# Second-layer weights of a two-layer block: converted inside the first layer's passes, in half chunks, instead of beside attention

## The chip, the cores and the metric

The kernel runs on one core of a Trainium2 chip. A core has a matrix engine (PE, with its weight loads listed apart as PEld), a vector engine (DVE), an activation engine (ACT), a general engine (POOL) and a queue engine (SP) that issues the DMAs. Each engine runs its own instructions in order; between engines only semaphores order the work. Matrix products land in PSUM, everything else lies in SBUF or, in DRAM, in tensors of the kernel.

The metric is the device time of one execution in microseconds (us). The kernel before takes 1280.64 us, the median of three runs (1280.03 to 1281.29).

## The reference

Two blocks follow each other. Attention over 64 pairs of batch and head (576 queries and keys of width 64), where only scores within `tau` of the row's maximum are kept; then a feed-forward layer over the 4608 tokens, 512 to 2048 to 512, with a squared ReLU between.

```python
scores = 0.125 * q @ k.T                      # per batch and head
scores = where(scores >= max(scores) - tau, scores, -1e9)
attn   = softmax(scores) @ v                  # float32
x      = attn as (4608, 512)                  # heads side by side
h      = maximum(x @ w_in, 0)                 # w_in (512, 2048), float64 in DRAM
out    = (h * h) @ w_out                      # w_out (2048, 512), float64 in DRAM
```

The two weight matrices arrive as float64. The core computes in float32, so each weight is turned from the two 32-bit words of a float64 into a float32 by integer arithmetic on the engines.

## The kernel before, in words

The program has three stages, one after the other: attention, the first layer, the second layer.

**Attention** is a software pipeline of periods: `period(p)` works on two units of 128 queries, and the order of its steps is written out by hand as a list of names. There are two lists that matter here. `PLAIN` has the attention steps, and one step `s1` that adds or subtracts two weight tiles on POOL. `CONVERTING` has the attention steps and `c1` to `c6`, which convert one chunk of weights; a period takes this list when a chunk is under way in it (`converts(p)`). `starts` gives chunk m the periods m+2 and m+3. Each period has one reciprocal (L488), so their starts mark the periods in the trace.

A chunk is 128 rows of 512 float64 values, 512 KB. Its six steps are: the high words' absolute value on ACT (L208), a conversion of the low words on ACT (L214), a clamp on POOL (L221), a shift and mask on DVE (L229), a merge of sign and exponent bits on DVE (L237), and the sum of the two parts on POOL (L248). Before, 32 chunks are converted so: 16 of the first layer's matrix, which stay in SBUF (`wall`), and 16 of the second layer's, which are stored to a DRAM tensor `w` (L250), since SBUF has no room for them yet.

**Both layers** use a scheme with fewer products than the plain block product: a 4 x 4 split of the matrices is multiplied with 7 x 7 = 49 products of blocks in place of 64, and pays with sums and differences of blocks. `OUTER` is the order of the seven outer kinds. So each weight matrix is needed in 49 blocks: 16 raw ones and 33 made by subtracting. For the first layer they are made during attention by `sums` (44 sums, step `s1`; what is left at its end goes to DVE and into the first pass). For the second layer they are made in DRAM during the first layer by `chain_out`: a chain loads four blocks of a quarter's width from `w` (L1192), makes four new ones from them with four subtractions of 128 x 128 on POOL (L125) and stores these (L1197). There are 44 chains, 16 along one side (raw blocks only) and 28 along the other. In the last pass of the first layer, `reload` fetches the 49 finished blocks from `w` into `wall`.

**The first layer** runs nine passes (`PASSES`) of 49 products each. Three passes work on 512 tokens and six are halves of a 1024-token set. After each product comes a tick: `also` runs what is planned for that tick of the pass (weight chains, loads of later tokens, sums of later tokens), all in the program's order. One outer kind is seven products (`inner`): PE writes a product into one of six PSUM banks, and DVE adds it to what is there from before (L128, PSUM plus SBUF to SBUF, 128 x 512); the first of each seven is copied by ACT (L769). Some of the results go on to POOL, which adds them to the running sums (L128, SBUF plus SBUF, 128 x 512). PE writes the bank of the third product of the seven again at the sixth, and that of the fourth again at the seventh, so DVE has to have read them by then. Finished results are squared by ACT (L916, L917) and stored to DRAM by SP.

The sums of later tokens (`sum_v`) run on DVE too (L125), after ACT has copied one of the two operands into PSUM (L879, tile `c`). DVE thus reads one operand from PSUM and one from SBUF in all its work of this stage. POOL reads both operands from SBUF.

**The second layer** runs nine blocks of 49 products (L1085) with the weights in `wall`.

## Time and profile before

| what | value |
|---|---|
| time, median of three runs | 1280.64 us (1280.03 to 1281.29) |
| profiled execution, span of its instructions | 1278.6 us |
| attention, up to the first product of the first layer | 492.6 us |
| first layer, first to last product | 387.9 us |
| PE, share of the span | 98% |
| DVE, ACT, POOL, share of the span | 78%, 67%, 70% |
| granted PE clock | 1.00 |

The profile gives the profiled execution its span, 1278.6 us from its first instruction to its last; the 2.0 us between this and the median of the runs lie around it. Busy times of an engine are the time in which at least one of its instructions ran. In rows of groups the columns are line, engine, operation, output and inputs, shapes and count, then busy time in us and mean length of one in ns, then the engine's idle time just before and what ended it. Rows of windows give a stretch, its length, and for each engine the busy time in it with the count of its instructions.

### The profile page before, as it was taken

The numbers are of one execution on the slowest core, as the hardware profiler recorded it, in microseconds if no ns is written. First come the engines' busy times: TensorE is split into PE (matmuls) and PEld (weight loads), VectorE is DVE, ScalarE is ACT, GpSimd is POOL, SyncE is SP. The second block draws the span as 40 slices with busy tenths as digits, with TensorE's granted clock in tenths as the row PEclk, the third lists the DMA queues.
The fourth block names the chain that finished last, engine by engine and source line by source line (L and its number), as shares of the span: only waits on it lengthen the run. The fifth ranks groups of instructions, "written<-read, shape, count | busy, mean of one in ns | idle before, by whom it ended". The sixth has DMA issues, their size and how long they took to land.

```text
span 1278.6 us, 44201 instructions
## 1 busy us (share of the span) xinstructions
PE 1255.2 (98%) x17459; PEld 1087.0 (85%) x17459; DVE 1000.2 (78%) x2449; ACT 855.6 (67%) x1552; POOL 897.4 (70%) x1094
## 2 busy tenths in 40 slices
PE   8999999999999999999999999999999999999998
PEld 6666666677777768988888888999999999999998
DVE  6999999999999997787878877877645664565463
ACT  6999999999999995666765767667422441343240
POOL 2565665655555557888798889858877777786775
PEclk9999999999999999999999999999999999999999
DMA  6566666544333413457666666589635414522511
GB/s 155 152 158 160 165 193 182 151 94 112 89 83 84 97 34 98 156 164 219 198 190 204 192 198 187 177 324 394 208 122 166 133 50 149 166 95 76 161 35 34
DMA packets 256591, 191.89 MB, mean 150 GB/s; under 512 B 96000, under 2 KB 217344, under 8 KB 256384
## 3 DMA queue, kind: packets, MB, share of 16 engines
q1 hardware_dynamic: 254928, 188.63, 49.8%
q8 instruction: 137, 2.24, 0.7%
q14 instruction: 70, 0.57, 0.1%
q10 hardware_dynamic: 1456, 0.44, 0.1%
HBM read 116.65 MB, written 72.35 MB: 148 GB/s over the span
## 4 chain that ended last, share of the span: by engine, by line
PE 70%; DMA 1%; ACT 1%; DVE 1%; issue 1%; ACTq 0%; DVEq 0%; SPq 0%
PE po L1085 30%; PE ph L946 27%; PE sc L544 5%; PE sc L445 4%; PE pt L388 2%; DMA wall<-w 1%; PE sc L406 1%; PE sc L388 1%; DVE arena L128 1%; DVE arena L463 0%; DMA g<-arena 0%; ACT arena L916 0%; ACT c L879 0%; DMA arena<-xT 0%; ACT arena L917 0%
## 5 line engine op out<-in xcount | busy, mean ns | idle before, releaser
L128 POOL TENSOR_TENSOR arena<-arena 128x512 f32<-128x512 f32 (+1 forms) x314 | 377.7, 1222 | 126.3 <-DVE arena L128 89.4
L1085 PE MATMUL po<-wall,arena 128*128 128x128 f32 x3528 | 394.4, 275 | 0.2 <-DVE arena L125 0.2
L1085 PEld LDWEIGHTS po<-wall,arena 128*128 128x128 f32 x3528 | 394.1, 192 | 0.4 <-DVE arena L125 0.4
L946 PE MATMUL ph<-arena,wall 128*128 128x128 f32 (+1 forms) x2352 | 387.4, 327 | 1.1 <-DVE arena L665 0.5
L946 PEld LDWEIGHTS ph<-arena,wall 128*128 128x128 f32 x2352 | 354.2, 191 | 34.2 <-DVE arena L128 2.2
L128 DVE TENSOR_TENSOR arena<-ph,arena 128x512 f32<-128x512 f32 x378 | 255.6, 688 | 75.8 <-PE ph L946 50.0
L125 POOL TENSOR_TENSOR arena<-arena 128x128 f32<-128x128 f32 (+2 forms) x314 | 255.2, 814 | 29.1 <-DMA arena<-w 10.7
L879 ACT COPY c<-arena 128x512 f32<-128x512 f32 (+2 forms) x319 | 176.1, 558 | 104.2 <-DVE arena L125 85.7
L473 ACT ACTIVATE arena<-arena 128x576 f32<-128x576 f32 x288 | 232.1, 918 | 16.7 <-DVE arena L463 16.7
L128 DVE TENSOR_TENSOR arena<-po,arena 128x128 f32<-128x128 f32 x378 | 108.3, 290 | 168.0 <-PE po L1085 167.4
L478 DVE SCALAR_TENSOR_TENSOR arena<-arena 128x576 f32<-128x576 f32 x288 | 225.5, 811 | 0.4 <-POOL arena L470 0.4
L463 DVE TENSOR_SCALAR_CACHE_REDUCE arena<-sc 128x576 f32<-128x576 f32 x288 | 204.5, 751 | 14.3 <-ACT arena L535 6.4
L125 DVE TENSOR_TENSOR arena<-arena,c 128x512 f32<-128x512 f32 (+2 forms) x283 | 176.8, 633 | 7.9 <-ACT c L879 6.1
L544 PEld LDWEIGHTS sc<-arena 64*64 64x64 f32 x5760 | 144.4, 133 | 43.1 <-DVE arena L463 39.1
L445 PE MATMUL sc<-arena 64*64 64x64 f32 (+1 forms) x2304 | 170.0, 415 | 0.3 <-DVE arena L665 0.3
L544 PE MATMUL sc<-arena 64*64 64x128 f32 (+1 forms) x5760 | 160.8, 262 | 8.5 <-DVE arena L463 5.8
L535 ACT COPY arena<-pt 128x1024 f32<-128x1024 f32 x144 | 166.0, 1153 | 1.6 <-PE pt L388 1.5
L769 ACT COPY arena<-po 128x128 f32<-128x128 f32 x63 | 16.6, 264 | 185.4 <-PE po L1085 185.4
L388 PEld LDWEIGHTS pt<-ident,arena 64*128 64x128 f32 x2304 | 83.0, 138 | 41.7 <-ACT arena L535 33.8
L388 PE MATMUL pt<-ident,arena 64*128 64x64 f32 x2304 | 100.8, 227 | 2.4 <-ACT arena L535 2.1
L445 PEld LDWEIGHTS sc<-arena 64*64 64x64 f32 x2304 | 62.5, 132 | 47.5 <-issue 22.7
L470 POOL TENSOR_SCALAR arena<-arena,tau_p 128x2 f32<-128x2 f32 x144 | 65.5, 455 | 41.8 <-DVE arena L463 35.2
(51 smaller groups left out, 936.6 us busy)
## 6 DMA issues: line engine op xcount, KB each, us to landing
g<-arena SPq DMA_DIRECT2D x144, 256.0 KB, 2.6
arena<-g SPq DMA_DIRECT2D x144, 256.0 KB, 4.5
w<-arena SPq DMA_DIRECT2D x60, 256.0 KB, 2.8
wall<-w SPq DMA_DIRECT2D x49, 256.0 KB, 5.3
arena<-w SPq DMA_DIRECT2D x44, 256.0 KB, 3.1
arena<-in_v_dram SPq DMA_DIRECT2D x32, 288.0 KB, 4.6
out_dram<-arena SPq DMA_DIRECT2D x70, 128.0 KB, 2.4
arena<-in_q_dram SPq DMA_DIRECT2D x64, 128.0 KB, 4.1
```

Source lines behind the costliest of these rows:

```text
L125: e.tensor_tensor(out=out, in0=x, in1=y, op=ALU.subtract)
L128: e.tensor_tensor(out=out, in0=x, in1=y, op=ALU.add)
L388: made = nc.tensor.transpose(pt[:, r, ts(slot, HALF)], of[rows, :], ident[rows, rows])
L445: made = nc.tensor.matmul(sc[at, ds(to, count)], lhs, kT[rows, ds(at_k, count)], start=True, stop=True)
L463: made = nc.vector.tensor_scalar(out=s[:, j, :], in0=sc[:, ds(at, S)], scalar1=1.0, scalar2=None, op0=ALU.mult, op1=ALU.min, accum_out=nmx ...
L473: nc.scalar.activation(out=w[:, :, j, :], in_=of(j), func=AF.Exp, bias=nmx[:, j : j + 1], scale=-1.0)
L478: nc.vector.scalar_tensor_tensor(out=w[:, :, j, :], in0=of(j), scalar=thr[:, j : j + 1], in1=w[:, :, j, :], op0=ALU.is_le, op1=ALU.mult, a ...
L535: touch("weights", nc.scalar.copy(joined(to), whole(pt, 0, count)), at, 2 * BANK, m)
L544: made = nc.tensor.matmul(sc[ds(u * D, D), ds(5 * j * BANK + row, count)], loaded_v[i][rows, (c - (u != j)) % CH, :], wT[m][rows, ds(weigh ...
L879: nc.scalar.copy(c, y)
L946: nc.tensor.matmul(to[:, j, :], W_IN[m, k][:, ts(h * parts_ + j, P)], x_of(m, k), start=(not more and j == 0), stop=True, skip_group_check ...
L1085: nc.tensor.matmul(to, g[:, j, :], w[:, j, :], start=(not more and j == 0), stop=(j == 3), skip_group_check=True)
```

## The change

All conversion of the second layer's matrix leaves attention: only the 16 chunks of the first layer are left there, so the last `CONVERTING` period is the 17th of these and not the 33rd, and `PLAIN` periods follow 16 periods sooner.

In the first layer's passes a new function `half_step` converts the matrix in 32 half chunks, one each ten ticks from tick 8 on (`EVERY`). A half chunk is four raw blocks at one place along the other side, 64 columns wide, 128 x 256 values in all. In order of ticks: 0, absolute value and low words on ACT; 1, clamp, shift and mask, and merge, all three on DVE, from SBUF to SBUF; 2, the sum on POOL; 3, the load of the next half by SP; 4, the store of the four raw blocks and a copy of three of them into PSUM (`c`) by ACT; 5, three differences or sums on DVE that make the four new blocks; 6, their store. The loads have one buffer (`raw_w`), the results one each (`new_w`, `made_w`).

The 16 chains along the first side go, since the half steps make these blocks. The 28 others stay, at new ticks (92 to 368 and not 153 to 367), and their four subtractions are arranged another way. `RAW` and `MADE`, the places of the blocks in `w`, are reordered to suit.

```diff
-    RAW, MADE = (7, 1, 3, 2), (7, 5, 6, 4)
+    RAW, MADE = (1, 7, 2, 3), (5, 7, 4, 6)
...
-    blocks_out = [(m, k) for k in RAW for m in RAW]
-    chunks += [(W_OUT, m, k, out_blocks[m, k]) for m, k in blocks_out[:EARLY]]
...
-    starts = {m + 2: m for m in range(16 + EARLY)}
+    starts = {m + 2: m for m in range(len(chunks))}
...
+        def half_step(j, s_):
+            lo, hi = (raw_w.rearrange("p m (c two) -> p m c two", two=2)[:, :, :, z] for z in range(2))
+            bits = new_w.bitcast(I32)
+            if s_ == 0 and is_wide:
+                nc.scalar.activation(out=new_w, in_=hi.bitcast(FP32), func=AF.Abs)
+                nc.scalar.activation(out=lo, in_=lo.bitcast(U32), func=AF.Copy, bias=0.0, scale=2.0**-29)
+            if s_ == 1 and is_wide:
+                low, high = (0x38000000, 0x47EFFFFF)
+                nc.vector.tensor_scalar(
+                    out=new_w, in0=new_w, scalar1=as_float(high), scalar2=as_float(low), op0=ALU.min, op1=ALU.max
+                )
+                nc.vector.tensor_scalar(
+                    out=bits, in0=bits, scalar1=3, scalar2=0x3FFFFFFF, op0=ALU.logical_shift_left, op1=ALU.bitwise_and
+                )
+                nc.vector.scalar_tensor_tensor(
+                    out=hi, in0=hi, scalar=-(1 << 30), in1=bits, op0=ALU.bitwise_and, op1=ALU.bitwise_or
+                )
+            if s_ == 2 and is_wide:
+                nc.gpsimd.tensor_tensor(out=bits, in0=hi, in1=lo, op=ALU.add)
+            if s_ == 3 and j + 1 < len(halves_w):
+                load_half(j + 1)
+            if s_ == 4:
+                nc.sync.dma_start(out=to_w(0, j), in_=new_w)
+                c = b_pool.tile([P, BANK], FP32, tag="b", name="c")[:, 0 : 3 * HALF_C].rearrange("p (m c) -> p m c", m=3)
+                nc.scalar.copy(c, new_w[:, 0:3, :])
+                where_w[j] = c
+            if s_ == 5:
+                c = where_w.pop(j)
+                minus(nc.vector, made_w[:, 0:2, :], new_w[:, 1:4:2, :], c[:, 0:2, :])
+                plus(nc.vector, made_w[:, 3, :], made_w[:, 1, :], c[:, 0, :])
+                minus(nc.vector, made_w[:, 2, :], c[:, 2, :], made_w[:, 3, :])
+            if s_ == 6:
+                nc.sync.dma_start(out=to_w(4, j), in_=made_w)
...
-        chains = [((0, RAW.index(k)), c) for k in RAW for c in range(4)]
-        chains += [((1, made_at(m)), c) for c in range(4) for m in OUTER]
-        BEGINS = (0, 6, 12, 18, 24, 43)
-        CHAINS = [49 * n + BEGINS[c] for n in range(NSTEP - 1) for c in range(3 if n == 0 else 0, 6)][0 : len(chains)]
+        chains = [(made_at(m), c) for c in range(4) for m in OUTER]
+        CHAINS = [92 + 80 * c + (11, 11, 11, 6)[c] * i for c in range(4) for i in range(7)]
...
         def chain_out(n, tick):
 
+            j, s_ = divmod(49 * n + tick - 8, EVERY)
+            if 0 <= j < len(halves_w):
+                half_step(j, s_)
```

More of the change, by code (lines that the diff above doesn't have):

```diff
@@ L106 @@
     sb, cv = Region(arena, 0, X_AT[0]), Region(arena, X_AT[0], ARENA)
-    ident = const.tile([P, P], FP32, name="ident")
+    second = const.tile([P, BANK + BANK // 2], FP32, name="second")
+    ident = second[:, 0:P]
     make_identity(nc, ident)
@@ L184, in fetch @@
         src = chunks[m][3]
-        if not is_wide and m < 16:
+        if not is_wide:
             nc.sync.dma_start(out=weight(m)[:, :], in_=src)
@@ L245, in convert6 @@
         raws.pop(m)
[L246 to L250 removed]
+        nc.gpsimd.tensor_tensor(out=weight(m)[:, :].bitcast(I32), in0=hi, in1=lo, op=ALU.add)
     by = [nc.gpsimd]
@@ L1172, in reload @@
             nc.sync.dma_start(out=t[:, :], in_=w_dram[ds(at * P, P), :])
+        HALF_C = P // 2
+        halves_w = [(c, k, e) for c in range(4) for k in RAW for e in range(2)]
+        EVERY = 10
+        raw_w = second[:, ds(BANK // 2, BANK)].bitcast(I32).rearrange("p (m c) -> p m c", m=4)
+        made_w = second[:, 0 : BANK // 2].rearrange("p (m c) -> p m c", m=4)
+        new_w = arena[:, ds(17 * BANK + BANK // 2, BANK // 2)].rearrange("p (m c) -> p m c", m=4)
+        wide_w = moe_w_out.bitcast(I32) if is_wide else moe_w_out
@@ new lines, with to_w, load_half @@
+        from_w = wide_w.rearrange("(a b q p) (c d o) -> b q d p a c o", a=2, b=2, q=4, p=P, c=2, d=2)
+        where_w = {}
+        def to_w(kinds, j):
+            c, k, e = halves_w[j]
+            return w_slots[:, ds(kinds, 4), raw_at(k), ds(c * P + e * HALF_C, HALF_C)]
+        def load_half(j):
+            c, k, e = halves_w[j]
+            b, d = next((b, d) for b in range(2) for d in range(2) if AT_B[b][d] == k)
+            n = HALF_C * (2 if is_wide else 1)
+            from_ = from_w[b, c, d][:, :, :, ds(e * n, n)]
+            to = raw_w if is_wide else new_w
+            for a in range(2):
+                nc.sync.dma_start(out=to[:, ds(2 * a, 2), :], in_=from_[:, a, :, :])
```

28 lines of the change are left out of this document (6 added, 22 removed).

## The prediction

> **What bounds the kernel now.** I read the page first, then windows over attention and over the first layer, then the groups of the first layer by form.
>
> ```profile
> span 1278.6 us, 44201 instructions
> PE 1255.2 (98%) x17459; PEld 1087.0 (85%) x17459; DVE 1000.2 (78%) x2449; ACT 855.6 (67%) x1552; POOL 897.4 (70%) x1094
> ```
>
> PE is nearly always busy, but that doesn't mean PE sets the pace everywhere: where PE waits for another engine its matmuls only stand further apart. So I go by stage. Two stretches of attention follow, the first within the converting periods, the second within the plain ones (columns: PE, PEld, DVE, ACT, POOL); the two rows below them count the reciprocals in the same stretches, one per period.
>
> ```profile
> 38.60:248.60 210.00, 199.75 (x4824) 140.22 (x4819) 208.10 (x601) 209.81 (x368) 127.10 (x210) 1.00 0.65 171
> 255.50:475.30 219.80, 218.28 (x5606) 158.17 (x5602) 211.26 (x631) 209.49 (x356) 121.82 (x212) 1.00 0.37 86
> ```
>
> ```profile
> 38.60:248.60 210.00, 5.12 (x30) 1.00 0.65 171
> 255.50:475.30 219.80, 6.04 (x35) 1.00 0.37 86
> ```
>
> A converting period takes 210.0/30 = 7.00 us, and ACT is busy for 209.81 of 210.00: ACT is the bound there. A plain one takes 219.8/35 = 6.28 us, with PE at 218.28 of 219.80. In the first layer PE sets the pace, and this is how much room the others have in the stretch in which the half steps will run (ticks 8 to 324; the cuts fall between stretches with many and with few sums of later tokens):
>
> ```profile
> 499.60:568.40 68.80, 68.77 (x478) 64.57 (x477) 56.30 (x93) 41.94 (x80) 59.89 (x69) 1.00 0.48 153
> 568.40:594.20 25.80, 25.80 (x121) 22.70 (x120) 18.30 (x31) 19.60 (x37) 21.17 (x24) 1.00 0.77 225
> 594.20:654.40 60.20, 59.84 (x276) 51.65 (x275) 50.28 (x82) 38.82 (x73) 52.19 (x68) 1.00 0.61 184
> 654.40:680.20 25.80, 25.80 (x121) 22.73 (x120) 18.64 (x31) 19.59 (x37) 21.16 (x25) 1.00 0.72 225
> 680.20:740.40 60.20, 60.06 (x278) 52.28 (x277) 50.65 (x83) 39.24 (x75) 52.84 (x68) 1.00 0.60 184
> 740.40:774.80 34.40, 34.40 (x161) 30.27 (x161) 24.77 (x39) 22.54 (x40) 28.99 (x36) 1.00 0.75 230
> sum 275.20, PE 274.67 PEld 244.20 DVE 218.94 ACT 181.74 POOL 236.24; mean PE 45.78 PEld 40.70 DVE 36.49 ACT 30.29 POOL 39.37
> ```
>
> DVE has 275.20 - 218.94 = 56.3 us left, and most of that outside the three stretches with sums; POOL is busy for 86%. Who waits there:
>
> ```profile
> DVE arena L128 <- PE ph L946: 31.9, 70, 1.2
> PEld ph L946 <- DVE arena L128: 1.8, 4, 0.5
> ACT c L879 <- DMA arena<-xT: 11.3, 3, 6.0
> ```
>
> DVE waits for PE, hardly ever PE for DVE. Once DVE's work passes its window this turns round, since DVE must empty a bank within two products and can't work ahead.
>
> **Part 1, attention.** Sixteen periods (19 to 34) turn from converting to plain: 16 x (7.00 - 6.28) = 11.5 us less. Each loses the two ACT conversions, a clamp and a sum on POOL, two DVE operations, a 512 KB load and a store on SP; none is moved to another place of attention. The sums of the first layer's weights begin sooner, on POOL, which has 98 of 219.8 us free in plain periods; so fewer are left for the first pass. I cost this at nothing.
>
> **Part 2, what a half step costs DVE.** Rows for the same operations at 512 columns, one of nearly no columns for the fixed part, and the one shape that the first layer already has at 128:
>
> ```profile
> L229 DVE TENSOR_SCALAR arena<-arena 128x512 int32<-128x512 int32 x32 | 13.5, 423 | 0.0
> L237 DVE SCALAR_TENSOR_TENSOR arena<-arena 128x512 int32<-128x512 int32 x32 | 22.2, 693 | 0.0
> L119 DVE TENSOR_SCALAR qscale<-tau_c 128x1 f32<-128x1 f32 x1 | 0.2, 154 | 5.3 <-DMA tau_c<-in_tau_dram 5.3
> L125 DVE TENSOR_TENSOR arena<-arena,c 128x128 f32<-128x128 f32 x4 | 1.1, 278 | 0.0
> 615.61 0.67 DVE L125 TENSOR_TENSOR arena<-arena,c 128x512 f32<-128x512 f32 x1
> 616.21 0.68 DVE L128 TENSOR_TENSOR arena<-ph,arena 128x512 f32<-128x512 f32 x1
> ```
>
> At 256 columns, halfway to the fixed 154 ns: clamp and shift (423+154)/2 = 289 ns each, merge (693+154)/2 = 424; the three of tick 5: 278, and twice (278+154)/2 = 216. Together 1.71 us. The next instruction starts some 0.08 us before the last one ends (616.21 against 615.61 + 0.67), twice per half step: 1.55 us.
>
> To this comes what the operations wait for. Clamp, shift and merge read and write SBUF alone while POOL works there too; nothing in the first layer does so now on DVE. The trace shows such pairs in attention alone:
>
> ```profile
> L478 DVE SCALAR_TENSOR_TENSOR arena<-arena x288: 783/810/1006, 12.8 to 484.7; 128x576 f32<-128x576 f32 x144
> 27.73 1.01 DVE L478 SCALAR_TENSOR_TENSOR arena<-arena 128x576 f32<-128x576 f32 x1
> L682 POOL TENSOR_TENSOR arena<-arena x72: 449/460/929, 27.2 to 492.5; 128x128 f32<-128x128 f32 x72
> 27.19 0.93 POOL L682 TENSOR_TENSOR arena<-arena 128x128 f32<-128x128 f32 x1 [0.83 <-ACT arena L667]
> 488.90 2.15 DVE L125 TENSOR_TENSOR wall<-wall 128x512 f32<-128x512 f32 x3
> ```
>
> The POOL addition at 27.19 takes 0.93 in place of 0.46, having begun under a DVE mask; it ends at 28.12, and the mask that started at 27.73 takes 1.01 in place of 0.81. So each holds the other up: DVE by 0.20 us where POOL had 0.39 to go. The three sums at 488.90 take 2.15 us, not the 0.60 + 0.60 + 0.68 = 1.88 that undisturbed spacing gives. In the first layer POOL's operations are longer:
>
> ```profile
> L128 POOL TENSOR_TENSOR arena<-arena 128x512 f32<-128x512 f32 x133 | 167.8, 1278 | 28.4 <-DVE arena L128 12.2 <-ACT c L879 10.7 <-ACT arena L917 2.8
> L125 POOL TENSOR_TENSOR arena<-arena 128x128 f32<-128x128 f32 x146 | 66.8, 460 | 10.5 <-DMA arena<-w 5.3
> ```
>
> What is left of the one that the clamp meets is on average (133 x 1.278^2 + 146 x 0.460^2) / (2 x (167.8 + 66.8)) = 0.53 us, met in 86% of cases: 0.45 us if the whole is waited for, 0.23 if half. I take 0.35. Shift and merge depend on the operation just before, so POOL may slip in again: nothing up to 1.28 us each. I take the 0.20 that was measured. In all w = 0.75 us per half step, between 0 and 0.45 + 2 x 1.28 = 3.0.
>
> The Trainium skill, in "SBUF — State Buffer", "Who interferes with whom", says that a vector instruction with two SBUF inputs or in a two-port mode and a GpSimd one lock each other out, the second until the first has ended. The measured 0.20 of 0.39 us is half of that; what the sum would be by the rule is the second rival.
>
> **Part 3, what this does to the pace.** Each stretch gets one half step per 8.6 us: 8, 3, 7, 3, 7 and 4 of them, each 1.55 + 0.75 = 2.30 us. DVE's work less the stretch: 56.30 + 18.4 - 68.8 = 5.9; 18.30 + 6.9 - 25.8 < 0; 50.28 + 16.1 - 60.2 = 6.2; again < 0; 50.65 + 16.1 - 60.2 = 6.6; 24.77 + 9.2 - 34.4 < 0. PE loses 18.6 us. That lateness can wait a product or two makes it less, that work clumps within a stretch makes it more; I let these cancel.
>
> **Part 4, ACT, POOL, SP.** ACT gets three operations:
>
> ```profile
> L214 ACT ACTIVATE arena<-arena 128x512 int32<-128x512 uint32 x32 | 32.9, 1028 | 0.0
> L208 ACT ACTIVATE arena<-arena 128x512 f32<-128x512 f32 x32 | 32.2, 1011 | 0.0
> L879 ACT COPY c<-arena 128x256 f32<-128x256 f32 x36 | 13.2, 376 | 37.2 <-DVE arena L125 26.0 <-DMA arena<-xT 11.3
> 697.40:714.60 17.20, 16.82 (x31) 1.00 0.65 206
> sum 86.00, ACT 80.56; mean ACT 16.11
> ```
>
> About half of 1.01 and of 1.03, and under 0.38: 1.4 us. On average there is room (181.74 + 32 x 1.4 = 227 of 275.2). But around the end of a pass ACT is full with squares: the last two rows are the fullest of five such stretches of 17.2 us and their sum. With two half steps each they need 80.56 + 10 x 1.4 = 94.6 of 86.0, 8.6 us too much; there ACT's copy of the first of seven products comes late and DVE behind it. The DVE term already lengthens these stretches by 18.6 x 86/275 = 5.8, so 2.8 would be left. Between the bounds 0 and 8.6 I take 1.5 us, about half of what is left.
>
> POOL loses 16 chains of four subtractions, 64 x 0.46 = 29 us, and gets 32 sums of about half of this row, 24 us, nothing on balance:
>
> ```profile
> L248 POOL TENSOR_TENSOR arena<-arena 128x512 int32<-128x512 int32 x16 | 23.7, 1484 | 34.9 <-DVE arena L237 19.6 <-ACT arena L535 13.2 <-DMA xT<-arena 2.2
> L1197 SPq DMA_DIRECT2D w<-arena x44: 359/360/562, 521.6 to 826.8; - x44
> ```
>
> SP issues 128 DMAs more in the first layer (64 loads, 64 stores) and 32 fewer chain DMAs: 96 x 0.36 = 35 us of issue in 275. It waits at a load for POOL's sum and at a store for DVE's, with the stores of squares and loads of tokens queued behind; they have slack of several ticks, and I cost this at nothing. Where that cover is gone, ACT waits for a token load as it does three times now, at up to 6.0 us.
>
> **The sum**, against the profiled execution: 1278.6 - 11.5 + 18.6 + 1.5 = 1287.2. The median stands 2.0 us above that span: 1289.
>
> **Rivals.** *First, faster: the three DVE operations don't wait for POOL (w = 0).* For it: the shift and merge of attention have 0.0 us idle and even lengths. Then the stretches lack 56.30 + 12.4 - 68.8 < 0, 0.9 and 1.3, 2.2 in all; with 1.5 for ACT, -11.5 + 3.7 = -7.8: 1273. Against: the masks at 27.73. It decides below the w at which the loss is 10 us: the three full stretches give 2.1 + 22 w, so w = 0.36. *Second, much slower: POOL gets a whole operation in before each of the three.* Its mean is (167.8 + 66.8)/279 = 0.84 us, so w = 0.45 + 2 x 0.86 x 0.84 = 1.9; the six stretches lack 15.1, 2.9, 14.2, 3.2, 14.6 and 4.2, 54 us; -11.5 + 54 = +42.5, ACT's share within it: 1323. For it: POOL almost always has its next operation ready (only 12.2 us of waits for DVE). By the rule of the Trainium skill it is this one. *Third: attention isn't shorter*, should the periods after the 17th be held by loads or sums; +20.1: 1301. Against: the plain stretch does with them what is asked.
>
> **How the numbers follow.** A measurement tells 0.2%, 2.6 us, from no change. The forecast with w from 0.48 to 1.2 gives 1283 to 1302 and has 0.48; w from 0.24 to 0.48, within 2.6 us of before, 0.14; the first rival with w under 0.24 has 0.22; the second 0.11; the third 0.05. Faster 0.22, same 0.14, slower 0.64. Range 1272 to 1310: from the first rival to over the third, with most of the second left out.
>
> **What would show it.** Reciprocals after the 17th chunk period 6.28 us apart: part 1. Clamp and shift in the first layer at a mean well over 289 ns and merge over 424, with POOL's 128x512 sums over 1278: part 2. The first layer's products some 20 us longer than 387.9, with PE waiting for DVE (1.8 now): part 3. I am wrong if the three keep their bare lengths, if PE's waits name ACT or a DMA in DVE's place, or if attention does not end 11 us sooner.

## Result, and the profile after

The changed kernel takes 1338.68 us (median of four runs, 1337.59 to 1340.78) against 1280.97 for the kernel before (1280.03 to 1281.35): a ratio of 1.0447, 95% interval 1.0429 to 1.0466. It is slower, as forecast, but by 57.7 us where 8.4 were forecast, and outside the range.

The stages first, read from the profiled execution, which is the longest of the four. One window over a part of attention's plain periods and one over the first layer (columns: PE, PEld, DVE, ACT, POOL, each with its count of instructions; then the granted clock). The changed kernel:

```profile
183.90:246.70 62.80, 62.53 (x1606) 45.28 (x1600) 60.30 (x181) 60.21 (x104) 34.98 (x60) 1.00 0.37 85
484.46:940.91 456.45, 410.81 (x2354) 359.88 (x2355) 379.31 (x687) 285.19 (x566) 306.42 (x335) 0.97 0.64 194
```

and the first layer of the kernel before:

```profile
492.59:880.49 387.90, 387.37 (x2354) 354.35 (x2355) 305.65 (x495) 253.65 (x470) 326.47 (x378) 1.00 0.65 207
```

The first layer starts 8.1 us sooner (484.46 for 492.59) and lasts 456.45 us for 387.90, 68.5 more. From its end to the end of the span are 398.1 us in both (1339.0 - 940.91 and 1278.6 - 880.49). So -8.1 + 68.5 = +60.4 us of span, all of it in the first layer. There PE is idle for 45.6 us and busy for 23.4 us more with the same products.

Groups from the first layer of the changed kernel, between 488 and 940 us, by form (mean ns of one after the busy time, then the idle time before them and what ended it):

```profile
L930 PE MATMUL ph<-arena,wall 128*128 128x256 f32 x1176 | 276.1, 394 | 39.8 <-DVE arena L129 34.4 <-DVE arena L126 4.0 <-ACT arena L753 0.8
L129 POOL TENSOR_TENSOR arena<-arena 128x512 f32<-128x512 f32 x187 | 236.6, 1280 | 112.8 <-DVE arena L129 107.7 <-DMA w<-arena 1.2 <-ACT arena L901 1.0
L1192 DVE TENSOR_SCALAR arena<-arena 128x256 int32<-128x256 int32 x32 | 22.3, 698 | 1.1
L1195 DVE SCALAR_TENSOR_TENSOR second<-second,arena 128x256 int32<-128x256 int32 x32 | 19.0, 594 | 1.1
L1189 DVE TENSOR_SCALAR arena<-arena 128x256 f32<-128x256 f32 x32 | 18.4, 576 | 6.8 <-ACT arena L1185 6.7
```

Clamp (L1189), shift (L1192) and merge (L1195) take 576, 698 and 594 ns, and POOL's sums keep their 1280. Some of the longest waits of the same stretch (total us, times, longest; L1205 is ACT's copy of a half, L1199 POOL's sum):

```profile
POOL arena L129 <- DVE arena L129: 107.7, 68, 11.2
...
ACT c L1205 <- POOL arena L1199: 40.6, 19, 5.3
PE ph L930 <- DVE arena L129: 39.6, 29, 3.5
```

PE now waits for DVE's additions (L129), in pauses of up to 3.5 us. This is the turn that the prediction named, and its size is the surprise. One of the worst half steps of the changed kernel as the timeline has it (start, length, engine, operation; in brackets the idle time before and who ended it):

```profile
629.57 7.53 POOL L129 TENSOR_TENSOR arena<-arena 128x512 f32<-128x512 f32 x6 [0.15 <-DVE arena L129]
...
632.48 0.68 DVE L129 TENSOR_TENSOR arena<-ph,arena 128x512 f32<-128x512 f32 x1
...
633.42 1.27 DVE L1189 TENSOR_SCALAR arena<-arena 128x256 f32<-128x256 f32 x1 [0.26 <-ACT arena L1185]
...
634.73 1.25 DVE L1192 TENSOR_SCALAR arena<-arena 128x256 int32<-128x256 int32 x1
...
636.01 1.37 DVE L1195 SCALAR_TENSOR_TENSOR second<-second,arena 128x256 int32<-128x256 int32 x1
...
637.30 0.68 DVE L126 TENSOR_TENSOR arena<-arena,c 128x512 f32<-128x512 f32 x1
...
637.90 2.30 DVE L129 TENSOR_TENSOR arena<-ph,arena 128x512 f32<-128x512 f32 x3
...
639.43 2.93 PE L930 MATMUL ph<-arena,wall 128*128 128x256 f32 x6 [3.52 <-DVE arena L129]
```

POOL has six sums back to back, 7.53/6 = 1.26 us each, and each of the three DVE operations takes as long as one of them: here each waits until the running sum has ended. With a sum of later tokens (L126) behind the three, DVE empties no bank from 633.16 to 637.90, for 4.7 us, and PE stands still for 3.52.

### The profile page after: what moved, and what is told of

It is laid out like the page before. It is cut to its first block, busy times and chain, and to the rows that moved or that the text cites. A ratio compares the mean times of both kernels' runs of the same rounds, so it can differ in the third digit from the quotient of the medians.

```text
span 1339.0 us, 44458 instructions
## 1 busy us (share of the span) xinstructions
PE 1273.9 (95%) x17459; PEld 1091.7 (82%) x17459; DVE 1056.5 (79%) x2604; ACT 871.5 (65%) x1616; POOL 865.3 (65%) x1035
## 4 chain that ended last, share of the span: by engine, by line
PE 38%; DMA 4%; ACT 4%; DVE 4%; issue 3%; POOL 2%; SPq 0%; DVEq 0%; ACTq 0%; POOLq 0%
PE po L1069 29%; PE ph L930 9%; DVE arena L129 2%; DMA wall<-w 2%; ACT arena L900 2%; DMA g<-arena 2%; ACT arena L901 1%; POOL arena L129 1%; DMA w<-arena 1%; DVE arena L126 1%; ACT c L863 1%; POOL arena L126 0%; POOL arena L1199 0%; DVE arena L1189 0%; DMA arena<-w 0%
## 5 line engine op out<-in xcount | busy, mean ns | idle before, releaser
L129 POOL TENSOR_TENSOR arena<-arena 128x512 f32<-128x512 f32 (+1 forms) x314 | 378.7, 1224 | 194.5 <-DVE arena L129 175.3
L930 PE MATMUL ph<-arena,wall 128*128 128x128 f32 (+1 forms) x2352 | 410.8, 336 | 46.2 <-DVE arena L129 39.6
L930 PEld LDWEIGHTS ph<-arena,wall 128*128 128x128 f32 x2352 | 359.7, 195 | 97.2 <-DVE arena L129 56.3
L129 DVE TENSOR_TENSOR arena<-ph,arena 128x512 f32<-128x512 f32 x378 | 253.3, 687 | 53.1 <-PE ph L930 31.0
L126 POOL TENSOR_TENSOR arena<-arena 128x512 f32<-128x512 f32 (+1 forms) x250 | 226.7, 907 | 27.3 <-DMA arena<-w 10.6
L129 DVE TENSOR_TENSOR arena<-po,arena 128x128 f32<-128x128 f32 x378 | 108.4, 290 | 168.2 <-PE po L1069 167.9
L457 ACT ACTIVATE arena<-arena 128x576 f32<-128x576 f32 x288 | 220.5, 817 | 21.4 <-DVE arena L447 21.4
L126 DVE TENSOR_TENSOR arena<-arena,c 128x512 f32<-128x512 f32 (+2 forms) x283 | 177.0, 634 | 5.1 <-ACT c L863 4.0
L519 ACT COPY arena<-pt 128x1024 f32<-128x1024 f32 x144 | 152.2, 1057 | 2.9 <-PE pt L372 2.9
L753 ACT COPY arena<-po 128x128 f32<-128x128 f32 x63 | 16.6, 264 | 185.4 <-PE po L1069 185.4
L372 PEld LDWEIGHTS pt<-second,arena 64*128 64x128 f32 x2304 | 83.5, 139 | 49.9 <-ACT arena L519 44.1
L372 PE MATMUL pt<-second,arena 64*128 64x64 f32 x2304 | 100.4, 227 | 1.7 <-ACT arena L519 1.5
L454 POOL TENSOR_SCALAR arena<-arena,tau_p 128x2 f32<-128x2 f32 x144 | 71.8, 499 | 42.0 <-DVE arena L447 34.5
```

The costliest lines, as they stand in the source:

```text
L126: e.tensor_tensor(out=out, in0=x, in1=y, op=ALU.subtract)
L129: e.tensor_tensor(out=out, in0=x, in1=y, op=ALU.add)
L372: made = nc.tensor.transpose(pt[:, r, ts(slot, HALF)], of[rows, :], ident[rows, rows])
L457: nc.scalar.activation(out=w[:, :, j, :], in_=of(j), func=AF.Exp, bias=nmx[:, j : j + 1], scale=-1.0)
L519: touch("weights", nc.scalar.copy(joined(to), whole(pt, 0, count)), at, 2 * BANK, m)
L930: nc.tensor.matmul(to[:, j, :], W_IN[m, k][:, ts(h * parts_ + j, P)], x_of(m, k), start=(not more and j == 0), stop=True, skip_group_check ...
```

## Experiments

The first-layer price of each part was looked for by leaving parts of the half step out or giving them another place. "The stores alone" is the first run below; differences are between medians. No run's edit touches attention, yet in the profiled executions of the runs the first layer starts anywhere between 480.5 and 487.7 us. So a difference of a few us between medians says little unless the first layer itself shows it.

**Stores only.** All arithmetic of the half step goes, loads included; the two stores stay and write constants. (Here and below, a tile that nothing fills any more gets a constant once, ahead of the passes.)

```diff
-            if s_ == 0 and is_wide:
...
-            if s_ == 1 and is_wide:
...
-            if s_ == 2 and is_wide:
...
-            if s_ == 3 and j + 1 < len(halves_w):
-                load_half(j + 1)
             if s_ == 4:
                 nc.sync.dma_start(out=to_w(0, j), in_=new_w)
-                nc.scalar.copy(c, new_w[:, 0:3, :])
...
-            if s_ == 5:
...
```

> The half steps' loads, conversion, copy and differences are left out; their 64 stores to DRAM stay and store constants (so the second layer's weights are not the real ones). Attention is as in the changed kernel. Both theories: attention's gain of 11.4 us stands alone and the first layer takes about the 388 us of before, so 1268 to 1271 us. If the layer stays long, the later chains or the stores cost time, and neither theory holds.

1273.21 us (ratio 0.9938, 0.9914 to 0.9961). Attention is shorter, as forecast. The first layer takes 391.0 us, 3 more than before, with 2.5 us of pauses of PE, which puts the time 2 us above the forecast. So the arithmetic and the loads of the half steps cost 1338.7 - 1273.2 = 65.5 us, 2.05 us for each of the 32.

**Without clamp, shift and merge** (tick 1 removed, all else kept).

```diff
-            if s_ == 1 and is_wide:
-                nc.vector.tensor_scalar(
...
-                nc.vector.tensor_scalar(
...
-                nc.vector.scalar_tensor_tensor(
...
```

> Clamp, shift and merge on DVE are left out, all else of the half steps stays (so the second layer's weights are not converted rightly). The port theory (DVE operations that use SBUF alone wait for POOL's and hold DVE up): nearly all of the loss goes, 1275 to 1290 us. The queue theory (ACT's copy of a half chunk waits for POOL's sum and holds up the copies behind it): POOL's sum still comes late, 1315 to 1330 us.

1305.29 us (1.0183, 1.0156 to 1.0211). The three operations are worth 33.4 us; 32 us over the stores alone are left without them. Neither theory's band holds that: half of the loss stays without any of the three.

**Copy, differences and their store later**: ACT's copy waits 40.6 us for POOL's sum, so it was moved to tick 7, with the differences at 8 and the store at 9.

```diff
                 nc.sync.dma_start(out=to_w(0, j), in_=new_w)
+            if s_ == 7:
                 nc.scalar.copy(c, new_w[:, 0:3, :])
...
-            if s_ == 5:
+            if s_ == 8:
                 c = where_w.pop(j)
...
-            if s_ == 6:
+            if s_ == 9:
                 nc.sync.dma_start(out=to_w(4, j), in_=made_w)
```

> ACT's copy of a half chunk, the differences and their store come three ticks later (ticks 7, 8, 9 in place of 4, 5, 6); nothing else is changed. The queue theory: POOL's sum is done by then, ACT's 40.6 us of waits for it go, and with them most of the loss, 1280 to 1300 us. The port theory: the three DVE operations wait as before, 1325 to 1337 us.

1330.27 us (1.0378, 1.035 to 1.0407). The wait is nearly gone, in the waits of this kernel:

```profile
ACT c L1206 <- POOL arena L1199: 2.0, 2, 1.3
```

Yet only 8.4 us come back for some 40 of waiting, as the port theory had it. One of the longest waits of the first layer was mostly covered.

**Clamp, shift and merge through PSUM.** The absolute value goes to a PSUM tile, clamp and shift stay in it, and the merge reads one operand from it: the form that the kernel uses for its sums.

```diff
-                nc.scalar.activation(out=new_w, in_=hi.bitcast(FP32), func=AF.Abs)
+                b = b_pool.tile([P, BANK], FP32, tag="b", name="c")[:, 0 : 4 * HALF_C].rearrange("p (m c) -> p m c", m=4)
...
+                nc.scalar.activation(out=b, in_=hi.bitcast(FP32), func=AF.Abs)
...
+                mid = b.bitcast(I32)
-                    out=new_w, in0=new_w, scalar1=as_float(high), scalar2=as_float(low), op0=ALU.min, op1=ALU.max
+                    out=b, in0=b, scalar1=as_float(high), scalar2=as_float(low), op0=ALU.min, op1=ALU.max
...
-                    out=bits, in0=bits, scalar1=3, scalar2=0x3FFFFFFF, op0=ALU.logical_shift_left, op1=ALU.bitwise_and
+                    out=mid, in0=mid, scalar1=3, scalar2=0x3FFFFFFF, op0=ALU.logical_shift_left, op1=ALU.bitwise_and
...
-                    out=hi, in0=hi, scalar=-(1 << 30), in1=bits, op0=ALU.bitwise_and, op1=ALU.bitwise_or
+                    out=hi, in0=hi, scalar=-(1 << 30), in1=mid, op0=ALU.bitwise_and, op1=ALU.bitwise_or
```

> ACT writes the absolute value to a PSUM tile; clamp and shift work there, and merge reads one operand from PSUM. All is computed. The port theory: the three no longer wait for POOL (each at 0.30 to 0.45 us, 1.2 us in sum against 1.87) and most of the loss goes, 1280 to 1300 us. The queue theory: 1325 to 1337 us. Against a clean reading: the PSUM tile comes from the ring of two that the sums of later tokens use, so ACT may wait for that ring more often.

1316.40 us (1.027, 1.0242 to 1.0298), 22.3 less, between the bands of the two theories. The groups of this kernel's first layer:

```profile
L1196 DVE TENSOR_SCALAR c<-c 128x256 int32<-128x256 int32 x32 | 13.8, 433 | 1.1
L1193 DVE TENSOR_SCALAR c<-c 128x256 f32<-128x256 f32 x32 | 13.6, 425 | 4.4 <-ACT c L1187 4.4
L1199 DVE SCALAR_TENSOR_TENSOR second<-second,c 128x256 int32<-128x256 int32 x32 | 13.6, 424 | 1.1
```

Clamp and shift are slower by themselves (425 and 433 ns, where the shortest in SBUF in the changed kernel take 282 and 293) and yet shorter than what they took with the waits for POOL.

**Both**, the diffs of the last two runs together, and then **the late copy without the three operations**, to see whether the late copy's 8 us hang on the three. The second of these, beside the moved copy:

```diff
-            if s_ == 1 and is_wide:
...
+            if s_ == 7:
                 nc.scalar.copy(c, new_w[:, 0:3, :])
```

> Both at once: clamp, shift and merge by way of PSUM, and copy, differences and their store three ticks later. All is computed. If the two costs add as measured alone (22 and 8 us): 1306 to 1311 us. If ACT's wait for POOL's sum is the next thing behind the port, more than that goes: 1285 to 1300 us.

> Clamp, shift and merge left out (so the weights aren't right) and copy, differences and store three ticks later. The 32 us that stay without the three operations over the stores alone (1305 against 1273) are either waits for POOL's sum (queue theory: 1278 to 1290 us) or bare work that ACT and DVE have no room for (room theory: 1298 to 1305 us).

1309.57 us (1.0216, 1.0186 to 1.0246) and 1308.09 (1.0204, 1.0175 to 1.0234). With PSUM the late copy still brings 7, as the sum of the two alone has it. Without the three operations the median is no better (1308.1 for 1305.3) and above both bands. The first layers, without the three and then with the late copy besides, show why:

```profile
481.98:905.70 423.72, 402.45 (x2354) 352.88 (x2355) 324.41 (x591) 285.12 (x566) 303.86 (x335) 0.99 0.69 209
```

```profile
487.71:907.51 419.80, 398.81 (x2354) 351.80 (x2355) 322.66 (x591) 283.74 (x566) 303.59 (x335) 1.00 0.70 211
```

The first layer is 3.9 us shorter with the late copy, but starts 5.7 us later. 3.9 of 32 us is little all the same: ACT's wait for POOL's sum is not what the 32 us are made of, and the queue theory falls there.

**Without copy and differences as well**: loads, ACT's two conversions, POOL's sum and the stores remain.

```diff
-            if s_ == 1 and is_wide:
...
             if s_ == 4:
                 nc.sync.dma_start(out=to_w(0, j), in_=new_w)
-                nc.scalar.copy(c, new_w[:, 0:3, :])
...
-            if s_ == 5:
...
```

> Of the half steps stay the loads, ACT's two conversions, POOL's sum and both stores (the second of constants); the three DVE operations, ACT's copy and the three differences are left out, so the weights aren't right. If the rest of the loss hangs on the copy and the differences (waits for POOL, 0.7 us of DVE): 1274 to 1282 us. If it hangs on ACT's two conversions (0.87 us, and waits for the store of the half chunk before): 1290 to 1300 us.

1292.51 us (1.0083, 1.0053 to 1.0112): copy and differences cost 12.8 us; ACT's two, POOL's sum and the loads 19.3 over the stores alone. The waits of this kernel:

```profile
ACT arena L1185 <- DMA w<-arena: 26.3, 18, 3.1
DVE arena L129 <- ACT arena L753: 26.2, 16, 4.2
```

ACT waits at tick 0 of a half for the store of the half before, and behind it stands the copy of the first of seven products (L753), for which DVE waits.

**Each DVE operation in a tick of its own**: clamp at 1, shift at 2, merge at 3, sum at 4, load at 5, store at 6, copy at 7 and on.

```diff
+            if s_ == 2 and is_wide:
                 nc.vector.tensor_scalar(
                     out=bits, in0=bits, scalar1=3, scalar2=0x3FFFFFFF, op0=ALU.logical_shift_left, op1=ALU.bitwise_and
...
+            if s_ == 3 and is_wide:
                 nc.vector.scalar_tensor_tensor(
...
-            if s_ == 2 and is_wide:
+            if s_ == 4 and is_wide:
                 nc.gpsimd.tensor_tensor(out=bits, in0=hi, in1=lo, op=ALU.add)
-            if s_ == 3 and j + 1 < len(halves_w):
+            if s_ == 5 and j + 1 < len(halves_w):
                 load_half(j + 1)
-            if s_ == 4:
+            if s_ == 6:
                 nc.sync.dma_start(out=to_w(0, j), in_=new_w)
```

> As the run with the late copy, but clamp, shift and merge at three ticks of their own (1, 2, 3), POOL's sum at 4, load and first store at 5 and 6; all in SBUF, all computed. If DVE is late because three waits for POOL come in a row: the longest hold-up falls from three POOL operations to one between two products, 1295 to 1312 us. If the sum of the waits counts and not their place: 1325 to 1332 us, as with the late copy.

1342.04 us (1.0469, 1.0439 to 1.05), outside both bands. Two waits grew:

```profile
ACT arena L1185 <- DMA w<-arena: 49.3, 23, 5.5
DVE arena L1189 <- ACT arena L1185: 32.5, 21, 5.1
```

The store, now at tick 6, lands too near the next absolute value, which writes the same tile, and ACT waits 49.3 us for it in place of 9.8, with everything behind it. So this run doesn't tell what spreading alone would bring.

**The wait for the store taken out**: as the run with ACT's two and POOL's sum, with the absolute value written to a PSUM tile that nobody reads.

```diff
-                nc.scalar.activation(out=new_w, in_=hi.bitcast(FP32), func=AF.Abs)
+                b = b_pool.tile([P, BANK], FP32, tag="b", name="c")[:, 0 : 4 * HALF_C].rearrange("p (m c) -> p m c", m=4)
+                nc.scalar.activation(out=b, in_=hi.bitcast(FP32), func=AF.Abs)
```

> As the run without the three DVE operations and without copy and differences, but ACT writes the absolute value to a PSUM tile that nothing reads, so that ACT no longer waits for the store of the half chunk before (26.3 us there, 18 times). The weights aren't right. If that wait makes ACT late: 1274 to 1282 us. If it is the bare 0.87 us of ACT and the sum on POOL: 1288 to 1293 us.

1289.02 us (1.0046, 1.001 to 1.0081), in the band of the bare work. The wait for the store is worth some 3.5 of the 19 us, a rough figure, since the three executions lie 5 us apart.

**The differences on POOL**, without ACT's copy, with the bits in PSUM (the diff of the run through PSUM belongs to it too), and the second store at tick 8.

```diff
-                nc.scalar.copy(c, new_w[:, 0:3, :])
...
-                minus(nc.vector, made_w[:, 0:2, :], new_w[:, 1:4:2, :], c[:, 0:2, :])
-                plus(nc.vector, made_w[:, 3, :], made_w[:, 1, :], c[:, 0, :])
-                minus(nc.vector, made_w[:, 2, :], c[:, 2, :], made_w[:, 3, :])
+                minus(nc.gpsimd, made_w[:, 0:2, :], new_w[:, 1:4:2, :], new_w[:, 0:2, :])
+                plus(nc.gpsimd, made_w[:, 3, :], made_w[:, 1, :], new_w[:, 0, :])
+                minus(nc.gpsimd, made_w[:, 2, :], new_w[:, 2, :], made_w[:, 3, :])
-            if s_ == 6:
+            if s_ == 8:
```

> By way of PSUM for clamp, shift and merge, and the three differences on POOL from SBUF, without ACT's copy. All is computed. Room theory: DVE's part falls from 2.0 to 1.3 us per half step, ACT's by 0.32: 1288 to 1302 us. If POOL's three operations more (about 1 us per half step) come to bound: 1305 us and more.

1307.62 us (1.0197, 1.0168 to 1.0227), 2 us below the other PSUM run with a late copy (1309.6). Work taken from ACT and DVE and given to POOL gains next to nothing.

**Ten of the 32 halves**, once in the stretches with few sums of later tokens (8 to 10, 18 to 20, 28 to 31), once in the full ones (5 to 7, 13, 15 to 17, 25 to 27); the other halves only load and store.

```diff
+            if j not in WORKED:
+                if s_ == 3 and j + 1 < len(halves_w):
+                    load_half(j + 1)
+                if s_ == 4:
+                    nc.sync.dma_start(out=to_w(0, j), in_=new_w)
+                if s_ == 6:
+                    nc.sync.dma_start(out=to_w(4, j), in_=made_w)
+                return
```

> Of the 32 half steps only ten do their work, those in the stretches without sums of later tokens (numbers 8 to 10, 18 to 20, 28 to 31); the others only load and store. The weights aren't right. Room theory: these ten fit, under 0.7 us each over the stores alone, 1273 to 1280 us. If every half step costs the same by its own waits (65 us over 32, 2.0 us each): 1291 to 1296 us.

> The same with ten half steps in the stretches with sums (numbers 5 to 7, 13, 15 to 17, 25 to 27). Room theory: they find DVE and ACT full, 3 us each, 1298 to 1310 us. If every half step costs the same: 1291 to 1296 us.

1291.51 us (1.0075, 1.0034 to 1.0115) and 1297.16 (1.0116, 1.0086 to 1.0145). Over the stores alone this is 18.3/10 = 1.8 us per half in the stretches with room and 24.0/10 = 2.4 in the full ones, with 2.05 as the mean of all 32. The first lies in the band of equal costs, the second between its two bands. Where DVE has most room a half step costs almost as much: it isn't the total of DVE's work in a stretch that sets the price.

**Each part alone on the stores.** The last question was whether the steps of this ladder (19, 13, 33 us) are each part's own price, or arise only since the others made DVE late already. Four runs keep the loads, the stores and one part: ACT's two conversions; POOL's sum; clamp, shift and merge from SBUF to SBUF; the same through PSUM. In all four the copy at tick 4 and the differences at tick 5 go; the first also drops ticks 1 and 2, the second ticks 0 and 1, the last two ticks 0 and 2. What stays of the second and of the fourth is changed so:

```diff
-                nc.gpsimd.tensor_tensor(out=bits, in0=hi, in1=lo, op=ALU.add)
+                nc.gpsimd.tensor_tensor(out=lo, in0=hi, in1=lo, op=ALU.add)
```

```diff
-                    out=new_w, in0=new_w, scalar1=as_float(high), scalar2=as_float(low), op0=ALU.min, op1=ALU.max
+                    out=b, in0=new_w, scalar1=as_float(high), scalar2=as_float(low), op0=ALU.min, op1=ALU.max
...
-                    out=bits, in0=bits, scalar1=3, scalar2=0x3FFFFFFF, op0=ALU.logical_shift_left, op1=ALU.bitwise_and
+                    out=mid, in0=mid, scalar1=3, scalar2=0x3FFFFFFF, op0=ALU.logical_shift_left, op1=ALU.bitwise_and
...
-                    out=hi, in0=hi, scalar=-(1 << 30), in1=bits, op0=ALU.bitwise_and, op1=ALU.bitwise_or
+                    out=hi, in0=hi, scalar=-(1 << 30), in1=mid, op0=ALU.bitwise_and, op1=ALU.bitwise_or
```

> Of each half step only the loads, the two ACT operations and the stores are left; nobody reads what ACT makes but the store. With the stores alone 1273.2 was measured, with ACT's two and POOL's sum 1292.5, of which some 3.5 are ACT's wait for the store. If ACT's two conversions hold up its copies of first products (ACT theory), this takes 1285 to 1292. If POOL's sum is what costs (POOL theory), 1275 to 1280.

> Of each half step only the loads, POOL's sum (written into the loaded half, not into the tile that is stored) and the stores are left. ACT theory: POOL has the room, its sum costs under 3 us, 1273 to 1276. POOL theory: 1280 to 1288.

> Of each half step only the loads, clamp, shift and merge on DVE from SBUF to SBUF, and the stores are left; they wait for no ACT. If the three cost by themselves as they did on top of the rest (own hold-ups), 33 us over the stores alone: 1300 to 1310. If they cost so much only because DVE was already late through the other parts (compounding), 1280 to 1292.

> As the run with clamp, shift and merge alone, with the middle result in PSUM, so that none of the three works between two SBUF tiles for long: each is bare. Own hold-ups: the price of 1.2 us of DVE time per half without port waits, 11 us over the stores alone as on top of the rest, 1281 to 1287. Compounding: 1274 to 1279. The difference to the SBUF form is the price of the waits for POOL alone, 22 us by the earlier pair.

| on the stores alone (1273.2) | time, us | ratio to before, 95% | added, us |
|---|---|---|---|
| ACT's two conversions | 1284.48 | 1.0018 (1.0004 to 1.0032) | 11.3 |
| POOL's sum | 1282.37 | 1.0002 (0.9988 to 1.0016) | 9.2 |
| clamp, shift, merge in SBUF | 1310.07 | 1.0219 (1.0192 to 1.0246) | 36.9 |
| clamp, shift, merge through PSUM | 1285.48 | 1.0028 (1.0019 to 1.0038) | 12.3 |
| copy and differences (from the ladder) | | | 12.8 |

In the profiled executions the first layer alone is longer by 10.8, 9.0, 36.3 and 11.7 us, in the order of the table. Compounding falls for these parts: the three cost 36.9 alone and 33.4 on top of the rest, ACT and POOL 20.4 apart and 19.3 together. With copy and differences, which no run has alone, the parts make 11.3 + 9.2 + 36.9 + 12.8 = 70.2 us against the 65.5 of the whole. ACT's 11.3 us miss the ACT theory's band by half a us, and POOL's 9.2 lie in the POOL theory's: both parts of the first step pay.

Each of the four runs also has the loads, which the stores alone leave out. That these cost next to nothing by themselves is seen in the run with ten halves in the stretches with room. There the first eight halves only load and store, and up to 567 us PE has no pause but the half us ahead of the first product:

```profile
482.00:567.00 85.00, 84.47 (x579) 79.24 (x580) 68.17 (x112) 49.86 (x95) 47.00 (x38) 1.00 0.55 160
```

The three operations alone, groups of the run in SBUF:

```profile
L1189 DVE TENSOR_SCALAR arena<-arena 128x256 int32<-128x256 int32 x32 | 26.5, 827 | 1.1
L1192 DVE SCALAR_TENSOR_TENSOR second<-second,arena 128x256 int32<-128x256 int32 x32 | 19.8, 619 | 1.1
L1186 DVE TENSOR_SCALAR arena<-arena 128x256 f32<-128x256 f32 x32 | 18.1, 567 | 0.3 <-DMA w<-arena 0.2
```

and of the run through PSUM:

```profile
L1191 DVE TENSOR_SCALAR c<-c 128x256 int32<-128x256 int32 x32 | 13.8, 432 | 1.1
L1194 DVE SCALAR_TENSOR_TENSOR second<-second,c 128x256 int32<-128x256 int32 x32 | 13.6, 424 | 1.1
L1188 DVE TENSOR_SCALAR c<-arena 128x256 f32<-128x256 f32 x32 | 13.4, 418 | 0.0
```

Per half step DVE is held for 567 + 827 + 619 = 2.01 us in the one and 418 + 432 + 424 = 1.27 us in the other. The first 1.27 us cost 12.3/32 = 0.38 us of time; the next 0.74 cost 24.6/32 = 0.77, one for one. PE, DVE and ACT each run in order and PE can go on only as long as its next bank is empty. So the reading that fits is that a short hold-up fits into what DVE has in hand, and what goes beyond is lost whole; no run isolates this. That the hand is near 0.9 us (1.27 - 0.38) is an estimate from this pair. DVE is busy for 85% of the first layer in the one and for 84% in the other, so it isn't full in either.

POOL's sum alone hurts by a way through SP's queue. The next load of a half fills the tile that the sum reads, so SP waits at it for the sum, and the loads of later tokens (L821) stand behind it in the queue. One such place, with the stores alone:

```profile
589.01 1.41 SPq L821 DMA_DIRECT2D arena<-xT  x2
...
594.52 0.38 ACT L863 COPY c<-arena 128x256 f32<-128x256 f32 x1 [6.04 <-DMA arena<-xT]
```

and in the run with POOL's sum (L1185; L1179 is the load of a half):

```profile
587.35 0.46 POOL L126 TENSOR_TENSOR arena<-arena 128x128 f32<-128x128 f32 x1 [4.93 <-DMA arena<-w]
...
588.99 0.61 POOL L1185 TENSOR_TENSOR second<-second 128x256 int32<-128x256 int32 x1
...
589.63 1.26 SPq L1179 DMA_DIRECT2D second<-in_moe_w_out_dram  x2
...
596.60 1.64 SPq L821 DMA_DIRECT2D arena<-xT  x2
...
602.03 0.38 ACT L863 COPY c<-arena 128x256 f32<-128x256 f32 x1 [8.71 <-DMA arena<-xT]
...
602.98 1.13 PE L930 MATMUL ph<-arena,wall 128*128 128x256 f32 x4 [2.30 <-ACT arena L753]
```

A chain's subtraction on POOL waits 4.93 us for its own load. The sum stands behind it and ends at 589.60, and only then SP issues the load of the half; it had ended the DMA before at 586.09. Counted from the first product (481.5 and 484.0 us), the tokens are asked for 5.1 us later (112.6 for 107.5) and ACT's copy of them comes 5.0 later. PE then stands still for 2.30 us. The 5 us are over half of the 9; the rest was not traced. In the whole changed kernel ACT waits only 3.8 us for tokens, where it waits 11.8 with the stores alone. So POOL's 9 us can't be carried over to the whole by this way, and that the sum of the parts comes near the whole may in part be chance.

## Why the prediction was wrong

**Part 1 was right.** Ten plain periods in 62.80 us, 6.28 each, follow where the kernel before has converting ones. The reciprocals of the 18th and the 36th period in the changed kernel, and in the kernel before (first and last start are the numbers ahead of the semicolon):

```profile
L472 DVE RECIPROCAL arena<-arena x1: 164/164/164, 139.6 to 139.6; 128x4 f32<-128x4 f32 x1
...
L472 DVE RECIPROCAL arena<-arena x1: 173/173/173, 253.1 to 253.1; 128x4 f32<-128x4 f32 x1
```

```profile
L488 DVE RECIPROCAL arena<-arena x1: 173/173/173, 136.8 to 136.8; 128x4 f32<-128x4 f32 x1
...
L488 DVE RECIPROCAL arena<-arena x1: 174/174/174, 261.9 to 261.9; 128x4 f32<-128x4 f32 x1
```

From 139.6 against 136.8 to 253.1 against 261.9: 2.8 us late turns into 8.8 early (261.9 - 253.1), a gain of 11.6 for the 11.5 forecast. That it stands 2.8 us late there wasn't foreseen, and the first layer starts only 8.1 us sooner for it. 2.1 of the 2.8 arise in the first two periods of the profiled execution, where the granted clock is 0.72 between 22 and 26 us, for 1.00 in the kernel before; no run was spent on why.

**Part 2 was right in its sum, in part by luck.** Clamp, shift and merge take 576 + 698 + 594 = 1.87 us against 289 + 289 + 424 = 1.00 bare: w = 0.87 us, forecast 0.75. The bare lengths were well estimated, as the shortest of each show (shortest, median and longest in ns behind the count):

```profile
L1189 DVE TENSOR_SCALAR arena<-arena x32: 282/498/1347, 494.3 to 831.6; 128x256 f32<-128x256 f32 x32
...
L1192 DVE TENSOR_SCALAR arena<-arena x32: 293/362/1331, 494.6 to 832.2; 128x256 int32<-128x256 int32 x32
...
L1195 DVE SCALAR_TENSOR_TENSOR second<-second,arena x32: 425/428/1374, 494.9 to 832.5; 128x256 int32<-128x256 int32 x32
```

Over these the three wait 0.29, 0.40 and 0.17 us on average, where 0.35, 0.20 and 0.20 were taken. Of the 96 operations 53 keep their bare length. Each of the other 43 started while POOL worked, and took what POOL's operation had left, less 0.13 to 0.15 us, on top: nearly the whole and not half of it. But the clamp has to wait in 18 of 32 cases, not in 86%. POOL's 128 x 512 sums keep their mean length in the rows (1280 for 1278), so that sign didn't show. The Trainium skill's rule in "SBUF — State Buffer", "Who interferes with whom", that DVE and GpSimd keep each other out for a whole instruction, is what the trace shows at 633.42 to 637.38, where each operation is as long as a POOL sum; but over all 32 halves w is 0.87 and not the 1.9 of the second rival, since 53 of the 96 don't wait.

**Part 3 failed.** The step is the sum by stretches: DVE's work against 26 to 69 us of time, with "I let these cancel" for lateness and clumping. By that sum the run through PSUM (1.27 us per half) lacks nothing in any stretch: 56.30 + 8 x 1.27 = 66.5 of 68.8, 50.28 + 7 x 1.27 = 59.2 of 60.2, 50.65 + 8.9 = 59.5 of 60.2. It measured 12.3 us. The run in SBUF (2.01 us) lacks 56.30 + 16.1 - 68.8 = 3.6, 4.2 and 4.5, 12.3 in all; it measured 36.9. DVE can't use the free time of a stretch later on, since PE waits within two products. So the DVE term is 36.9 for the three, and with the differences and ACT's copy for them 49.7, where 18.6 was forecast; and it isn't bound to the full stretches, as the ten halves with room show (1.8 us each).

**Part 4 failed in the same way.** ACT's 1.5 us were the shortfall of its fullest stretches; the two conversions measured 11.3, above the bound of 8.6 as well. They run ahead of ACT's copy of a first product, and DVE waits for that (18.8 us in the run with ACT alone). From its groups:

```profile
L129 DVE TENSOR_TENSOR arena<-ph,arena 128x512 f32<-128x512 f32 x376 | 253.4, 688 | 78.7 <-PE ph L930 38.4 <-ACT arena L753 18.8 <-ACT c L863 5.4
```

POOL was costed at nothing on balance, since it loses 29 us of work and gets 24; its sum alone measured 9.2, over half of it by way of the wait of SP that the prediction names ("it waits at a load for POOL's sum", with loads of tokens queued behind) and put at nothing. For the issue of loads and stores by itself nothing was right: with the stores alone PE's pauses are 2.5 us in all, and the first eight halves of the run with ten in the stretches with room, which only load and store, add none.

**The rivals.** The time lies above the second rival's 1323, yet not by its mechanism: w is less than half of what it needs. The first rival (w = 0) isn't what happens; and the runs through PSUM show that without any wait of the three for POOL (and 0.27 us more of bare time per half) the whole change still takes 1309 to 1316, where that rival had 1273. The third falls with part 1.

**What the sum had not at all**: the clock. In the changed kernel it is 0.97 over the first layer, 1.00 before: 0.03 x 456 is some 14 us (the rounding leaves it between 11 and 16), the larger part of PE's 23.4 us of longer work. The share of it that is lost time can't be told apart from the pauses here.

No version that computes everything was found to be faster than the kernel before. The stores alone bound what the move can gain at 8 us, and the cheapest single part already costs 9.

## What to carry to other kernels

Room on an engine over tens of microseconds says little where another engine waits for it every two products: cost each insertion by how long it holds the queue at once, against what that queue has in hand, and on every engine that hands results on, ACT and POOL too. Look also at what stands in a DMA queue behind a load that has to wait for its tile. Here, alone, 0.6 us more on POOL and 0.9 us more on ACT cost 0.29 and 0.35 us of time each (9.2/32, 11.3/32), and the three DVE operations between SBUF tiles beside a busy POOL took about twice their bare time (1.87 us for 1.00). A wait that ranks high in the list may still be covered: moving the 40 us one brought 8.

## What the runs showed of the hardware that was not expected

Long pauses of PE lower its clock. Windows of 4 us in the changed kernel around the pause of 3.52 us that ends at 639.43 (PE busy, its matmuls, granted clock):

```profile
637.00:641.00 4.00, 1.57 (x4) 0.71 0.27 79
641.00:645.00 4.00, 4.00 (x11) 0.50 1.03 299
645.00:649.00 4.00, 4.00 (x19) 0.94 0.62 180
```

After the pause PE is busy for all of 4 us and gets 11 matmuls done in place of 19 or 20. If the clock is either full or half, the three rows hold 2.3 + 4.0 + 0.5 = 6.8 us at half: from 638.7, which is 2.8 us into the pause, to 645.5, after 6.1 us of work. The Trainium skill, "TensorE: Matmul & The Clock Gate", "What's actually happening", has half the clock after an idle window of about 3.4 us and the full one again after a busy one of that length. The trace agrees on the size, since 6.8 us are two such windows, but a full idle window isn't needed: PE still worked for 0.6 of the 3.4 us ahead of the drop. Pauses of PE in the timeline around 585 us, and the clock behind them:

```profile
584.63 1.13 PE L930 MATMUL ph<-arena,wall 128*128 128x256 f32 x4 [1.71 <-DVE arena L129]
587.94 12.29 PE L930 MATMUL ph<-arena,wall 128*128 128x256 f32 x48 [2.18 <-DVE arena L129]
```

```profile
584.00:588.00 4.00, 1.19 (x5) 0.93 0.08 22
588.00:592.00 4.00, 4.00 (x12) 0.64 0.88 249
592.00:596.00 4.00, 4.00 (x20) 1.00 0.82 258
```

Two pauses of 1.71 and 2.18 us with 1.13 us of work between them were enough for 0.56 + 2.88 = 3.4 us at half the clock, and 12 matmuls in 4 us. So a pause costs its own length and, when it is long or another is near, half of the work of the next 3 to 6 us as well.
